# One order for all transfers, an earlier second inverse, and narrowing moved between engines, in a fused RWKV-7 and SoLU kernel

## The chip, the cores and the metric

One core of one Trainium2 chip. The metric is device time in microseconds (us) of one execution; medians are over three or more runs. Each kernel's times are set against runs of the kernel before on the same chip in the same session, as a ratio: the medians of the kernel before are 728.7 to 732.0 us from session to session, so a difference between the medians of two experiments of different sessions is good to some 2 or 3 us.

## The reference, cut to what matters

```python
batch, n_heads, seq, head_dim = (4, 8, 768, 40)
for t in range(S):                                   # attention block
    y[:, :, t] = np.einsum('bhd,bhde->bhe', rt, state)
    Sa = np.einsum('bhde,bhe->bhd', state, at)
    state = state * wt[:, :, None, :] - np.einsum('bhd,bhe->bhde', Sa, bt) + np.einsum('bhd,bhe->bhde', vt, kt)
# then, on the (3072, 320) result x, d_ff = 1024:
h = x @ w_in
solu = h * softmax(h)
out = ((solu - mu) / np.sqrt(var + 1e-06) * g_ln) @ w_out
```

`w_in` and `w_out` arrive as 64-bit floats; the kernel fetches their bits and narrows them to fp32 itself.

## The kernel before

The sequence is cut into 12 chunks of 64 steps, each done in two **rounds** (24 rounds). A chunk needs the inverse of a triangular matrix. Its blocks go to DRAM and come back in another layout (`scatter`, `gather`), VectorE inverts them in 30 steps of two instructions (`invert`), and the inverse goes out and back the same way (`bring_inverse`). The dense block (`hidden`, `output`) runs six rounds behind, once the weights are narrowed. Every engine, and SyncE's queue of transfers, does its instructions in the order that the program was written in; `turns` interleaves generators by a string of letters.

```python
def narrow(dst, land, tmp):                  # 26 pieces of weights
    ...
    yield
    nc.scalar.activation(out=scale, ...); nc.scalar.activation(out=frac, ...)
    nc.scalar.activation(out=rest, in_=low.bitcast(U32), func=AF.Copy, scale=2.0 ** -52)      # L169
    yield
    nc.vector.scalar_tensor_tensor(out=scale, in0=hi, ...)                                    # L171
    yield
    nc.gpsimd.tensor_tensor(out=frac, in0=frac, in1=rest, op=ALU.add)                         # L174
    nc.gpsimd.tensor_tensor(out=dst, in0=frac, in1=scale.bitcast(FP32), op=ALU.mult)          # L175
    yield
...
def front(i):        # ahead of the matmuls of round i
    nc.gpsimd.tensor_copy(out=keyed(a)..., in_=by_heads(given(i, "a")))                       # L361
def attend(i):
    nc.gpsimd.tensor_copy(out=lamv[:, :, :, L:], in_=given(i, "v")...)                        # L446
...
EARLY = ("r r a r W f r W W I r y W r W I a f a W s a f a W I W f s W I f a W L f", ...)      # rounds 0 to 5
STEADY = "r b r a r f b b o r o I o r o y o r I o h a f L a s a h f a I h f s h f h a f h"    # rounds 6 on
...                  # the loop over rounds, cut
if i % 2: gather((i + 3) // 2)
bring_inverse(i + 1)
if i % 2 == 0: load((i + 6) // 2, "w", "a"); parts["L"] = later((i + 6) // 2)   # L loads b, k
turns(...)
```

W is a step of narrowing, I a step of the inverse, f and g the fronts, a `attend`, r the recurrence, L the load of b and k. Small PSUM tiles come from one pool, `bank`, of two buffers that take turns: this matters below.

## Time and profile before

| | before |
|---|---|
| median of three runs | 730.19 us (728.36 to 730.9) |
| first inverse starts, ends (T0) | 24.3, 44.5 us |
| next three inverses end (T1, T2, T3) | 91.1, 151.4, 206.8 us |
| pu of round 0, round 7 starts | 56.6, 264.6 us |
| a pair of rounds in the steady stage | 47.5 us |

These are marks from the timeline: the copy to `ut` that ends each inverse, and the matmuls `pu`, one set a round. I use them throughout, as they cut the 728.0 us of the profiled execution into a start, a stage bound by latency (to about 265 us), a steady stage bound by TensorE, and a tail. Each kernel has one profile, so a mark has a spread too.

### The profile page before, as it was taken

What the parts mean: (1) busy time and instruction counts of PE and PEld (TensorE: products, weight loads), DVE (VectorE), ACT (ScalarE), POOL (GpSimd) and SP (SyncE); (2) the same over time, 40 slices, a digit from 0 to 9 for tenths busy, and PEclk for the clock granted to TensorE, in tenths of its full rate; (3) what the DMA queues carried; (4) which work ended last, traced back from release to release, by engine and by line L of the source; (5) the groups of instructions that cost most, each with busy time, mean ns of one, the idle gap of its engine ahead of it and who ended that gap; (6) DMA issues with size and microseconds to landing.
All of it is one profiled execution on the core that took longest, in us unless ns stands there. A gap on an engine that the chain in (4) does not pass through costs nothing.

```text
span 728.0 us, 25509 instructions
## 1 busy us (share of the span) xinstructions
PE 605.3 (83%) x10873; PEld 431.6 (59%) x10873; DVE 467.5 (64%) x1258; ACT 267.2 (37%) x631; POOL 128.5 (18%) x228
## 2 busy tenths in 40 slices
PE   6436636665766899999999999999999899979997
PEld 4325525554554766677667676767677666645554
DVE  3565945855854678868868688696786763233442
ACT  4114333443441344343524443345334343322322
POOL 4104131332330111220212111220111000000000
PEclk9657576775876799999999999999999999998999
DMA  8946374455444443563555546536315231000001
GB/s 143 160 81 113 72 163 84 83 117 111 92 93 98 67 97 72 103 120 69 100 98 91 101 79 114 102 62 131 71 31 104 53 60 34 21 24 18 19 5 32
DMA packets 269793, 59.84 MB, mean 82 GB/s; under 512 B 255464, under 2 KB 265328, under 8 KB 269680
## 3 DMA queue, kind: packets, MB, share of 16 engines
q1 hardware_dynamic: 265680, 52.73, 39.8%
q10 hardware_dynamic: 4000, 5.48, 2.9%
q8 instruction: 86, 1.41, 0.8%
q14 instruction: 27, 0.22, 0.1%
HBM read 40.08 MB, written 13.37 MB: 73 GB/s over the span
## 4 chain that ended last, share of the span: by engine, by line
PE 58%; DVE 22%; DMA 7%; issue 5%; ACT 4%; SPq 3%; POOL 1%; ACTq 0%; DVEq 0%; POOLq 0%
PE po L662 14%; PE h L617 12%; DVE prod L414 7%; DVE u L416 6%; PE pyo L589 4%; PE plnT L657 3%; PE pcx L341 2%; PE pcum L328 2%; DVE nmax L627 2%; PE plamv L280 2%; PE py L484 2%; DMA raw_b<-in_b_dram 2%; PE pyo L511 2%; PE pvT L261 2%; PE ppsi L280 1%
## 5 line engine op out<-in xcount | busy, mean ns | idle before, releaser
L617 PE MATMUL h<-w_in,xT 128*128 128x512 f32 (+1 forms) x288 | 128.2, 635 | 3.9 <-DVE e L634 3.9
L662 PE MATMUL po<-w,lnT 128*128 128x320 f32 x384 | 114.8, 438 | 0.0
L414 DVE TENSOR_TENSOR prod<-blk,u 128x30 f32<-128x30 f32 (+4 forms) x360 | 107.0, 297 | 11.8 <-DMA blk<-blk_dram 1.0
L416 DVE TENSOR_TENSOR u<-u,prod 128x30 f32<-128x30 f32 (+4 forms) x360 | 101.5, 282 | 12.4
L662 PEld LDWEIGHTS po<-w,lnT 128*128 128x128 f32 x384 | 68.8, 190 | 26.2 <-issue 2.9
L331 POOL TENSOR_TENSOR kx<-raw_b,inv 128x320 f32<-128x320 f32 x24 | 20.7, 866 | 254.8 <-ACT inv L329 210.1
L627 DVE TENSOR_REDUCE nmax<-h 128x1 f32<-128x1024 f32 x24 | 29.3, 1221 | 44.8 <-PE h L617 44.8
L617 PEld LDWEIGHTS h<-w_in,xT 128*128 128x128 f32 (+1 forms) x288 | 38.2, 191 | 31.6 <-issue 29.7
L484 PE MATMUL py<-tinv,nt 32*32 32x32 f32 x768 | 20.6, 202 | 34.2 <-DMA tinv<-ut_dram 34.2
L667 ACT ACTIVATE osb<-po,rs 128x320 f32<-128x320 f32 x24 | 12.7, 527 | 97.2 <-PE po L662 86.4
L596 DVE TENSOR_TENSOR x<-pyo,kx 128x512 f32<-128x512 f32 x24 | 16.6, 690 | 45.2 <-PE pyo L589 44.5
L282 DVE TENSOR_TENSOR lamv<-plamv,cst 128x512 f32<-128x512 f32 x24 | 16.5, 689 | 39.8 <-PE plamv L280 39.8
L649 POOL TENSOR_TENSOR rs<-c,mhalf 128x1 f32<-128x1 f32 x24 | 13.2, 548 | 158.4 <-DVE c L648 158.4
L658 ACT COPY lnT<-plnT 128x512 f32<-128x512 f32 x48 | 27.6, 586 | 33.8 <-PE plnT L657 33.5
L631 ACT ACTIVATE e<-h,nmax 128x1024 f32<-128x1024 f32 x24 | 26.7, 1114 | 36.1 <-DVE nmax L627 36.1
L484 PEld LDWEIGHTS py<-tinv,nt 32*32 32x32 f32 x768 | 17.2, 112 | 36.7 <-issue 29.3
L634 DVE TENSOR_TENSOR e<-h,e 128x1024 f32<-128x1024 f32 x24 | 29.4, 1225 | 14.6 <-ACT e L631 14.2
L499 ACT ACTIVATE tinvT<-pz 32x256 f32<-32x256 f32 x48 | 17.9, 372 | 56.9 <-PE pz L484 56.6
L341 PEld LDWEIGHTS pcx<-cst,lw 128*128 128x128 f32 x192 | 29.1, 209 | 14.9 <-ACT y_mid L496 8.5
L341 PE MATMUL pcx<-cst,lw 128*128 128x132 f32 x192 | 33.6, 307 | 5.3 <-ACT y_mid L496 3.4
L657 PE MATMUL plnT<-cst,e 128*128 128x128 f32 x192 | 29.9, 285 | 5.7 <-DVE e L634 5.4
L575 POOL TENSOR_TENSOR sm<-tot,fac 128x320 f32<-128x320 f32 x20 | 14.8, 742 | 95.2 <-DVE tot L574 79.2
(104 smaller groups left out, 1121.3 us busy)
## 6 DMA issues: line engine op xcount, KB each, us to landing
blk<-blk_dram SPq DMA_DIRECT2D x24, 256.0 KB
raw_w<-in_w_dram SPq DMA_DIRECT2D x24, 160.0 KB
raw_a<-in_a_dram SPq DMA_DIRECT2D x24, 160.0 KB
raw_b<-in_b_dram SPq DMA_DIRECT2D x24, 160.0 KB
raw_k<-in_k_dram SPq DMA_DIRECT2D x24, 160.0 KB
v<-in_v_dram SPq DMA_DIRECT2D x24, 160.0 KB
r<-in_r_dram SPq DMA_DIRECT2D x24, 160.0 KB
out_dram<-osb SPq DMA_DIRECT2D x24, 160.0 KB
```

The costliest lines, as they stand in the source:

```text
L341: nc.tensor.matmul(t[:, g * 132:g * 132 + 132], lhsT=pair(lw, 2 * j + g), rhs=cst[:, lo:lo + 132], start=True, stop=True)
L414: nc.vector.tensor_tensor(out=t, in0=nb[:, j:j + 1, j + 1:Q].to_broadcast([P, rows, m]), in1=u[:, 0:rows, j:j + 1].to_broadcast([P, rows, ...
L416: nc.vector.tensor_tensor(out=u[:, 0:rows, j + 1:Q], in0=u[:, 0:rows, j + 1:Q], in1=t, op=ALU.subtract)
L484: nc.tensor.matmul(t[quarter(out), c:c + Q], lhsT=lhs(p, g), rhs=rhs(p, g), start=True, stop=True)
L589: nc.tensor.matmul(t[half(p), c, g * W:g * W + used], lhsT=kb[half(c), j, 2 * g + p, :], rhs=lam[half(c), h % 2, h // 2, 0:used], start=i ...
L617: nc.tensor.matmul(h[:, j * 512:j * 512 + 512], lhsT=of_round[i // 2]["xT"][rows, kt, i % 2 * P:i % 2 * P + P], rhs=w_in[rows, 4 if kt == ...
L627: nc.vector.tensor_reduce(out=nmax, in_=h, axis=AX.X, op=ALU.max, negate=True)
L631: nc.scalar.activation(out=e, in_=h, func=AF.Exp, bias=nmax, accum_out=esum)
L634: nc.vector.tensor_tensor(out=q, in0=h, in1=e, op=ALU.mult)
L657: nc.tensor.transpose(out=t[:, j * P:(j + 1) * P], in_=q[:, f * P:(f + 1) * P], identity=ident)
L658: nc.scalar.copy(out=lnT[:, fs.start:fs.stop].rearrange("p f t -> p (f t)"), in_=t)
L662: nc.tensor.matmul(o[:, 0:DM], lhsT=lnT[:, f, :], rhs=w2[:, f, :], start=f == 0, stop=f == NF - 1)
```

## The change

The intent: put what the chain waits for ahead of bulk in one queue, use VectorE's idle time while the first inverse travels, and take work off GpSimd, beside whose multiplies a step on VectorE took 0.90 us instead of 0.28. The diff, cut to its core:

```diff
-        nc.scalar.activation(out=rest, in_=low.bitcast(U32), func=AF.Copy, scale=2.0 ** -52)
-        nc.gpsimd.tensor_tensor(out=frac, in0=frac, in1=rest, op=ALU.add)
-        nc.gpsimd.tensor_tensor(out=dst, in0=frac, in1=scale.bitcast(FP32), op=ALU.mult)
+        nc.vector.scalar_tensor_tensor(out=frac, in0=low.bitcast(U32), scalar=2.0 ** -52, in1=frac, op0=ALU.mult, op1=ALU.add)
+        nc.vector.tensor_tensor(out=dst, in0=frac, in1=scale.bitcast(FP32), op=ALU.mult)
 ...
-                nc.scalar.dma_start(out=to[row:row + part.shape[0]], in_=part)      # weights
+                nc.sync.dma_start(out=to[row:row + part.shape[0]], in_=part)        # three pieces ahead, not two
 ...
-        nc.gpsimd.tensor_copy(out=keyed(a)[:, :, :, 0:D], in_=by_heads(given(i, "a")))
+        nc.scalar.copy(out=keyed(a)[:, :, :, 0:D], in_=by_heads(given(i, "a")))
-        nc.gpsimd.tensor_copy(out=lamv[:, :, :, L:], in_=given(i, "v")...)
+        nc.scalar.copy(out=lamv[:, :, :, L:], in_=given(i, "v")...)
 ...
-    EARLY = ("r r a r W f r W W I r y W r W I a f a W s a f a W I W f s W I f a W L f", ...
+    EARLY = ("r r a W I r f W r r I W y r W a f L a I W s a f W a f I W s I f a W f", ...
 ...                       # start: both queues for the first loads; r, a and three pieces of weights ahead of scatter(0)
+        load(0, "w", "b", "a", by=both)
+        turns("f W g", {}, f=f, g=g, W=ws)
+        load(0, "r")
+        load(1, "a")
 ...                       # second inverse right behind the first
+        turns("I W I s s", dict(I=[6, 6]), s=so, I=inv, W=ws)
 ...                       # in the loop: the inverse comes back ahead of the next blocks and of bulk
+            if i == LAG:
+                steps(ws, 99)
+                parts["o"] = centre()          # centring; in the kernel before the last of the W steps, in round 5
+            if more and (i % 2 or i == 0):
+                bring_inverse(i + 1)
             if i % 2 and (i + 3) // 2 < NCH:
                 gather((i + 3) // 2)
+            if i % 2 and i + 2 < N:            # after the round
+                bring_inverse(i + 2)
```

More of the change, by code (lines that the diff above doesn't have):

```diff
@@ L164, in narrow @@
         nc.vector.tensor_scalar(out=man, in0=hi, scalar1=0xFFFFF, scalar2=None, op0=ALU.bitwise_and)
-        frac, rest = man.bitcast(FP32), low.bitcast(FP32)
+        frac = man.bitcast(FP32)
         yield
@@ L172, in narrow @@
                                        op1=ALU.bitwise_or)
-        yield
-        nc.gpsimd.tensor_tensor(out=frac, in0=frac, in1=rest, op=ALU.add)
-        nc.gpsimd.tensor_tensor(out=dst, in0=frac, in1=scale.bitcast(FP32), op=ALU.mult)
+        nc.vector.scalar_tensor_tensor(out=frac, in0=low.bitcast(U32), scalar=2.0 ** -52, in1=frac, op0=ALU.mult,
+                                       op1=ALU.add)
+        nc.vector.tensor_tensor(out=dst, in0=frac, in1=scale.bitcast(FP32), op=ALU.mult)
         yield
     def weights():
-        nc.scalar.dma_start(out=g_rows, in_=moe_g_ln.rearrange("(c p) -> c p", p=P))
+        nc.sync.dma_start(out=g_rows, in_=moe_g_ln.rearrange("(c p) -> c p", p=P))
         pieces, hw, hm = [], DFF // 2, DM // 2
@@ L201, in weights @@
                 land += [x[:, 0:256], x[:, 256:512]]
-            temps = [two.tile([P, 2, 256], I32, tag=tag, name="parts", bufs=1) for tag in ("osb", "parts")]
+            temps = [two.tile([P, 2, 256], I32, tag=tag, name="parts", bufs=n)
+                     for tag, n in (("osb", 1), ("parts", 1), ("xT", 4), ("xT", 4))]
         def fetch(j):
@@ L210, in fetch @@
             for part in parts:
-                nc.scalar.dma_start(out=to[row:row + part.shape[0]], in_=part)
+                nc.sync.dma_start(out=to[row:row + part.shape[0]], in_=part)
                 row += part.shape[0]
-        for j in range(2):
+        for j in range(3):
             fetch(j)
@@ L218, in weights, with centre @@
         for j, (dst, _) in enumerate(pieces):
-            new = None if exact else narrow(dst, land[j % 4], temps[j % 2])
-            for _ in range(2):
-                for part in (open_, new):
-                    if part:
-                        next(part)
-                if _:
-                    fetch(j + 2)
-                yield
-            open_ = new
-        for _ in range(2):
+            new = None if exact else narrow(dst, land[j % 4], temps[j % 4])
+            if new:
+                next(new)
+            yield
+            if new:
+                next(new)
             if open_:
                 next(open_)
+            fetch(j + 3)
+            yield
+            open_ = new
+        if open_:
+            next(open_)
+        yield
+    def centre():
         pg = bank("pg")
@@ L233, in weights @@
         nc.scalar.copy(out=g_col, in_=pg[:, 0:NF])
-        yield
         gb = two.tile([P, NF, P], FP32, tag="e", name="gb", bufs=1)
@@ L237, in weights @@
         yield
-        mean = bank("mean")
+        t = bank("mean")
         for c in range(NF):
-            nc.tensor.matmul(mean[:, 0:DM], lhsT=gb[:, c, :], rhs=w2[:, c, :], start=c == 0, stop=c == NF - 1)
+            nc.tensor.matmul(t[:, 0:DM], lhsT=gb[:, c, :], rhs=w2[:, c, :], start=c == 0, stop=c == NF - 1)
+        mean = two.tile([P, DM], FP32, tag="osb", name="mean", bufs=1)
+        nc.scalar.copy(out=mean, in_=t[:, 0:DM])
         yield
@@ L243, in weights @@
             nc.vector.scalar_tensor_tensor(out=w2[:, c, :], in0=w2[:, c, :], scalar=g_col[:, c:c + 1],
-                                           in1=mean[:, 0:DM], op0=ALU.mult, op1=ALU.subtract)
+                                           in1=mean, op0=ALU.mult, op1=ALU.subtract)
             if c % 2:
@@ L290, with load @@
     of_round = [dict() for _ in range(NCH)]
-    def load(n, *names):
+    def load(n, *names, by=(nc.sync, nc.sync)):
         if n >= NCH:
@@ L305, in load @@
             for c in range(2):
-                nc.sync.dma_start(out=to[half(c)], in_=ap[2 * c:2 * c + 2, :, n * L:(n + 1) * L, :]
+                by[c].dma_start(out=to[half(c)], in_=ap[2 * c:2 * c + 2, :, n * L:(n + 1) * L, :]
                                   .rearrange("b h t d -> t (b h) d"))
@@ L445, in attend @@
         lamv = d["lamv"] = wide("lamv", L + D, 2)
-        nc.gpsimd.tensor_copy(out=lamv[:, :, :, L:], in_=given(i, "v").rearrange("q (m z) d -> q z m d", z=2)[:, :, :, 0:D])
+        nc.scalar.copy(out=lamv[:, :, :, L:], in_=given(i, "v").rearrange("q (m z) d -> q z m d", z=2)[:, :, :, 0:D])
         kT = transposed("kT", d["kb"][:, 0])
@@ L690, in fronts @@
         return [j for j in ((4, 5) if i == 0 else (i + AHEAD,)) if j < N]
-    EARLY = ("r r a r W f r W W I r y W r W I a f a W s a f a W I W f s W I f a W L f",
-             "r r a r W f g r W W I r y W r W I a f g a W s a f g a W I W f g s W I f g a W L f g")
+    EARLY = ("r r a W I r f W r r I W y r W a f L a I W s a f W a f I W s I f a W f",
+             "r r a W I r f W r r I g W y r I W a f g L W a I a f g W I s a f g a W I f g s W I f g W I")
     STEADY = "r b r a r f b b o r o I o r o y o r I o h a f L a s a h f a I h f s h f h a f h"
-    front_of = {}
-    front_of = {}
-    front_of = {}
-    front_of = {}
     front_of = {}
@@ L714, in inverse_steps @@
     def inverse_steps(i):
-        if i < 3:
-            return [[8, 8, 8, 8], [0, 3, 4, 3], [6, 6, 5, 5]][i]
+        if i == 0:
+            return [3, 2, 2, 3, 3, 3, 3, 1]
         if i < LAG:
-            return [0, 5, 5, 4] if i % 2 else [5, 5, 4, 4]
+            return [0, 0, 6, 6, 5 if i < LAG - 1 else 2] if i % 2 else [4, 4, 4, 3, 0]
         return [0, 7, 7] if i % 2 else [6, 7, 5]
@@ L726 @@
     with tc.manual_schedule():
-        load(0, "w", "a", "b", "k")
-        f, g = front(0), front(1)
+        both = (nc.sync, nc.scalar)
+        load(0, "w", "b", "a", by=both)
+        load(0, "k", "v")
+        f, g, at, inv, so, ws = front(0), front(1), attend(0), invert(0), solve(0), weights()
         turns("f g", {}, f=f, g=g)
-        load(1, "w", "a")
+        load(1, "w")
+        turns("f W g", {}, f=f, g=g, W=ws)
+        load(0, "r")
+        load(1, "a")
+        turns("f f f f g g g g f g", {}, f=f, g=g)
+        f, g = front(2), front(3)
         turns("f g", {}, f=f, g=g)
+        scatter(0)
         load(1, "b")
-        turns("f f f f g g g g f g", {}, f=f, g=g)
-        scatter(0)
         gather(0)
-        load(0, "v", "r")
         load(1, "k")
-        f, g, at, inv, so, ws = front(2), front(3), attend(0), invert(0), solve(0), weights()
-        turns("f g f g f f g g", {}, f=f, g=g)
-        load(2, "w", "a", "b", "k")
-        turns("a a I a a W", dict(I=99), a=at, I=inv, W=ws)
+        turns("a f g W a a W f f a g g W a", {}, f=f, g=g, a=at, W=ws)
+        load(2, "w", "a")
+        turns("I f g f g I f g", dict(I=[8, 8]), f=f, g=g, I=inv)
+        load(1, "v", "r")
+        scatter(1)
+        load(2, "b", "k")
+        gather(1)
+        turns("I a", dict(I=99), a=at, I=inv)
         bring_inverse(0)
-        turns("a f g a f g f g", {}, f=f, g=g, a=at)
-        scatter(1)
-        gather(1)
-        load(1, "v", "r")
         begin(0)
-        turns("s s", {}, s=so)
         inv = inverses()
+        turns("I W I s s", dict(I=[6, 6]), s=so, I=inv, W=ws)
         after, before = None, None
@@ L752 @@
             m, more, js = i - LAG, i + 1 < N, fronts(i)
+            now = hidden(m) if m >= 0 else None
+            parts = dict(r=recurrence(i), y=readout(i), I=inv, W=ws, h=now, b=after, o=before)
+            if i == LAG:
+                steps(ws, 99)
+                parts["o"] = centre()
+            parts.update(zip("fg", (front_of[j] for j in js)))
+            if more:
+                parts.update(a=attend(i + 1), s=solve(i + 1))
+            if more and (i % 2 or i == 0):
+                bring_inverse(i + 1)
             if i % 2 and (i + 3) // 2 < NCH:
                 gather((i + 3) // 2)
-            now = hidden(m) if m >= 0 else None
-            parts = dict(r=recurrence(i), y=readout(i), I=inv, W=ws, h=now, b=after, o=before)
-            if i >= LAG:
-                steps(ws, 99)
-            parts.update(zip("fg", (front_of[j] for j in js)))
-            if more:
-                bring_inverse(i + 1)
-                parts.update(a=attend(i + 1), s=solve(i + 1))
             if i % 2 == 0:
@@ L767 @@
             if i % 2:
+                if i + 2 < N:
+                    bring_inverse(i + 2)
                 load((i + 3) // 2, "v", "r")
```

## The prediction

> **What bounds the kernel now.** I read the page first, then busy time by windows, then the chain of waits, then the timelines of the transfer queue and of VectorE. The page's slices cut the 728.0 us into stages (one digit is 18.2 us):
>
> ```profile
> PE   6436636665766899999999999999999899979997
> DVE  3565945855854678868868688696786763233442
> DMA  8946374455444443563555546536315231000001
> ```
>
> TensorE is at 9 from slice 15 on, and at 3 to 7 before it. The windows put numbers to that:
>
> ```profile
> core 0: us, PE busy (x) PEld busy (x) DVE busy (x) ACT busy (x) POOL busy (x), PEclk, DMA share, GB/s
> 45.00:57.00 12.00, 8.37 (x184) 7.10 (x188) 4.24 (x9) 3.99 (x10) 0.00 (x0) 0.64 0.47 84
> 57.00:93.00 36.00, 22.33 (x436) 18.16 (x428) 29.58 (x87) 14.44 (x37) 11.07 (x15) 0.71 0.51 98
> 93.00:127.00 34.00, 17.13 (x399) 14.26 (x392) 17.25 (x48) 12.68 (x33) 10.66 (x15) 0.70 0.61 122
> 127.00:153.00 26.00, 18.51 (x404) 15.11 (x396) 22.07 (x65) 11.70 (x33) 9.30 (x16) 0.67 0.37 74
> 318.00:365.00 47.00, 46.09 (x916) 32.85 (x915) 36.33 (x97) 19.39 (x45) 7.96 (x14) 1.00 0.50 91
> ```
>
> From about 270 us two rounds take 47.5 us and TensorE is busy 46.1 of 47: that stage is bound by matmuls which the change leaves alone. Before it no engine is full; the chain there is latency. So **the change can win only ahead of about 265 us**. My milestones, from the timeline, are the ends of the inverses (the copy to ut, L420) at 44.5, 91.1, 151.4, 206.8 and 261.2 us, and the starts of the matmuls pu (L550), one set a round, at 56.6, 92.4, 126.5, 153.1, 184.8, 208.5, 244.7 and 264.6. Inverse ends are 60.3 and 55.4 us apart here, against 47.5 later. The queue of SyncE shows why:
>
> ```profile
> 91.13 0.54 SPq L423 DMA_DIRECT2D u_dram<-u  x1
> 91.79 0.59 SPq L425 DMA_DIRECT2D ut_dram<-ut  x1
> 92.43 0.55 SPq L423 DMA_DIRECT2D u_dram<-u  x1
> 93.07 2.38 SPq L306 DMA_DIRECT2D raw_b<-in_b_dram  x2
> 95.55 3.62 SPq L306 DMA_DIRECT2D raw_k<-in_k_dram  x2
> 99.26 2.74 SPq L389 DMA_DIRECT2D blk_dram<-nt  x4
> 103.49 1.12 SPq L396 DMA_DIRECT2D blk<-blk_dram  x2
> 109.32 1.79 SPq L436 DMA_DIRECT2D tinv<-ut_dram  x4
> 111.16 1.93 SPq L439 DMA_DIRECT2D tinvT<-u_dram  x4
> ```
>
> The inverse goes out at 91.1 to 93.0 and comes back only from 109.3, with raw_b, raw_k and the next blocks between. The next inverse waits for blk and starts at 107.1, 16 us after the last ended; pu of round 2, which needs tinvT, starts at 126.5, 35.4 us after. A second loss is on VectorE:
>
> ```profile
> 31.33 0.28 DVE L416 TENSOR_TENSOR u<-u,prod 128x120 f32<-128x120 f32 x1
> 31.65 0.90 DVE L414 TENSOR_TENSOR prod<-blk,u 128x114 f32<-128x114 f32 x1
> L174 POOL TENSOR_TENSOR parts<-parts,bits 128x160 f32<-128x160 f32 (+1 forms) x26 | 16.5, 636 | 3.4 <-ACT bits L169 3.4
> L175 POOL TENSOR_TENSOR w_in<-parts 128x256 f32<-128x256 f32 x10 | 8.3, 829 | 28.9 <-DVE parts L171 28.5
> ```
>
> A step of the inverse takes 0.28 us alone and 0.90 where a GpSimd multiply (from 31.56) runs beside it.
>
> **What the Trainium skill says.** "SBUF — State Buffer", section "SBUF: two separate sides": VectorE, when it has two SBUF inputs, and GpSimd lock one port pair for a whole instruction, and the loser blocks. The trace agrees: 0.28 to 0.90. Summing, over VectorE's instructions ahead of 245 us, duration less the shortest of the same shape, 13.3 us fall on those beside the narrowing's L174 and L175, and about 3.4 on those beside L331. "DMA: Bandwidth & Descriptors", section "Issuing engines are not separate DMA queues": transfers of all issuing engines interleave on the same 16 DMA engines, and several issuers save issue time alone. So one queue loses no bandwidth as such; what the change decides is who stands ahead of whom. Same page, "Queues, rings and completion order": descriptors are consumed in ring order. The trace agrees: in the first 17 us the 160-byte packets of seven loads run back to back at about 1,030 a us (1 us for each half of a load), and the first blocks' 128-byte packets start only behind them.
>
> **Part by part.**
> (1) Start. In the order of instructions, the changed kernel sends k, v, the second w, three pieces of weights (128 packets of 2 KB each, about 1 us a piece in the packet rates), r and the second a ahead of the first blocks: 16 halves and three pieces, about 19 us, against 14 halves now. Further, ScalarE, now the copier of a, stands in order ahead of lw of the second front, of kT, vT and rT, so it waits there for the second a. Working: loads from 2.4 us; a, spread over two queues, lands at about 9.5; the second w waits for lw (10.5); the second a lands at about 22; then ScalarE has some fourteen pieces of 0.4 to 0.6 us up to rT, 28.5; lamv on VectorE, which the order puts ahead of the first inverse, 30.5 to 31. So the first inverse starts at about 31, not 24.3: +6.7 us. In it now stand two kx and two nt (4 x 0.68 = 2.7), which before lay in the shadow of the return trip: it ends at 54.4, not 44.5. Return and solve as before, 12.1 us: first pu at 66.5, +10 us.
> (2) Second inverse. In those 12 us VectorE was busy 4.24; now it does the set-up (1.2), 14 of the 30 steps (about 8) and parts of narrowing. From lamu (70.5) to the end of the inverse remain sixteen steps (9), x, sm, psi, lamv, two kx, two nt (5.3) and some four pieces of narrowing (7): 22, with stalls 25. So T1 is about 96 against 91.1: **what is won here does not quite pay for the start**.
> (3) Inverse ahead of bulk. After T1: u and ut out (2), four scatters (2), eight returns at 0.48 (4), blk (1.1 and about 3 to land): the third inverse starts at T1 + 12 instead of + 16. VectorE from T1 to T2, by its order: a bare inverse 18.7, two rounds' own products 9.0, narrowing 11.6 (seven pieces of 0.47 to 0.57 and 0.93 to 1.22): 39.3. Of these 6.7 fit ahead of T1 + 12; 32.6 follow, at 87% busy (now 85% in 127 to 153): 37. T2 - T1 = 49 against 60.3. The same for T3 - T2: 13.5 to the start, 30 of work after it, 48 against 55.4. T3 is 96 + 97 = 193 against 206.8.
> (4) Narrowing. 26 pieces lose 33 us of GpSimd, 9.6 of ScalarE (L169) and 13.3 of contention. VectorE gains a multiply-add (0.41 or 0.31, as L171) and a multiply (about 0.4 or 0.31, by the slope of L414): 10 x 0.81 + 16 x 0.62 = 18. For VectorE that is a net cost of 5, so no gain in itself. It is spread thinner, about 3.5 pieces a round against 5.5 to 6, and three pieces are left for the start of round 6.
> (5) Centring. The mean (L240, 6.1 us of TensorE at 217.8, all on the chain) leaves round 5 and goes into round 6, behind its pu, with 8 x 0.54 of VectorE. From T3 to pu of round 7 I get 33 (three late pieces included) and 25 (19.9 now, plus some 5): 58, as now (57.8).
> Sum: pu of round 7 at 193 + 58 = 251 against 264.6, a gain of 13.6, and the rest is the steady stage and the tail, unchanged: 716.6. I take 2.5 off, as the stalls that I left at today's share also fall when fewer weight transfers are issued by ScalarE (about 40 of 0.38 us): **714 us**.
>
> **The rivals.**
> (a) The slow start eats everything: if a lands later still or gather waits behind the weights, the first pu comes at 75 and the kernel at 725 to 732. For it speaks the DMA share of 0.79 and 0.90 in the first 45 us; against it, that the steps' hand-set counts look tuned to fit.
> (b) The start is no slower, because two queues carry the first loads faster (up to 1,300 packets a us elsewhere in the trace), and the filled return trip counts fully: T1 near 85, 703 to 706. For it: VectorE idle in that trip. Against: the a copy on ScalarE.
> (c) VectorE becomes the bound ahead of 250 us by its 5 us net and three late pieces; then pairs take 52 to 54 and the time is about 724.
> (d) ScalarE, with two more copies of 0.45 a round, delays TensorE in the steady stage. TensorE idles only 0.9 of 47 us there, so 0.2 us a round would cost 4: 718. Against: ScalarE is busy 19.4 of 47.
>
> **Range and chances.** The sum's weak terms are the start (+10, give or take 5) and each pair's 49 and 48 (give or take 4 each, correlated); together about 10 us. Low 700 is rival (b) with quicker pairs, high 728 is (a). The border for faster by over 2% is 715.6, close to the centre: 0.54 faster, 0.42 same, 0.04 slower.
>
> **What would show it.** Right: inverse ends near 54, 96, 145 and 193; returns of the inverse issued within 5 us after it goes out; VectorE's steps at 0.28 but beside L337 (kx); 47.5 us a pair after 270. Wrong: step 1, if the first inverse starts before 27; step 2, if T1 is below 90; step 3, if the return still waits behind loads or T2 - T1 is over 54; step 5, if round 6 takes over 32; the frame itself, if a pair in the steady stage leaves 47 to 48.

## The result, and the profile after

Median 721.54 us (718.5 to 724.68, 4 runs) against 729.3 in the same rounds; the ratio is 0.9892, 95% interval 0.9844 to 0.9940: 1.1% faster, clear of noise, but under 2% and so called the same. A ratio here and below is the mean time of one kernel's runs over that of the other's of the same rounds, so not quite the ratio of the medians.

| mark | before | predicted | after |
|---|---|---|---|
| first inverse starts | 24.3 | 31 | 31.8 |
| T0 | 44.5 | 54.4 | 52.7 |
| pu of round 0 | 56.6 | 66.5 | 64.0 |
| T1 | 91.1 | 96 | 90.1 |
| T2 | 151.4 | 145 | 140.5 |
| T3 | 206.8 | 193 | 193.3 |
| pu of round 7 | 264.6 | 251 | 248.1 |
| a pair in the steady stage | 47.5 | 47.5 | 48.7 |
| end of the profiled span | 728.0 | | 719.9 |

At pu of round 7 the changed kernel leads by 16.5 us, at the end by 8.1: **half of the gain is given back, most of it in the steady stage**, where nothing was meant to change. Rounds 7 to 19 took 285.8 us before (264.6 to 550.4) and take 292.6 now (248.1 to 540.7), 6.8 more; the other 1.6 go in the tail.

The page's busy times and slices after:

```profile
PE 606.7 (84%) x10873; PEld 428.9 (60%) x10873; DVE 468.7 (65%) x1310; ACT 275.1 (38%) x654; POOL 77.7 (11%) x128
PE   4524866767658899999999999999999899979997
DVE  2387969658656959687687596786876754232442
DMA  9964553743765353545554626545325131000001
```

GpSimd fell from 128.5 to 77.7 us, and TensorE's 13th slice rises from 6 to 8. Busy time by windows, for three of the stretches shown before (columns: window, its length, then busy time of PE, PEld, DVE, ACT, POOL, then clock, DMA share, GB/s):

```profile
45.00:57.00 12.00, 0.00 (x0) 0.00 (x0) 7.34 (x29) 2.53 (x7) 0.00 (x0) 0.50 0.84 164
93.00:127.00 34.00, 22.52 (x481) 18.46 (x484) 25.75 (x84) 11.82 (x31) 2.03 (x3) 0.70 0.43 84
318.00:365.00 47.00, 45.45 (x910) 32.36 (x910) 34.36 (x93) 20.24 (x49) 6.47 (x10) 1.00 0.52 95
```

In 45 to 57, the return trip of the first inverse before, TensorE now does nothing at all: the first inverse ends only at 52.7. In 93 to 127 VectorE is busy 25.75 us instead of 17.25, and TensorE 22.52 instead of 17.13: here the change wins. In 318 to 365 TensorE is busy 45.45 instead of 46.09. SyncE's queue around T1:

```profile
88.66 0.55 SPq L429 DMA_DIRECT2D u_dram<-u  x1
90.77 0.33 SPq L431 DMA_DIRECT2D ut_dram<-ut  x1
91.14 0.55 SPq L429 DMA_DIRECT2D u_dram<-u  x1
91.74 2.35 SPq L395 DMA_DIRECT2D blk_dram<-nt  x4
94.20 3.22 SPq L442 DMA_DIRECT2D tinv<-ut_dram  x4
97.52 1.88 SPq L445 DMA_DIRECT2D tinvT<-u_dram  x4
99.44 1.13 SPq L402 DMA_DIRECT2D blk<-blk_dram  x2
```

The inverse comes back from 94.2, 3.4 us after ut went out, where it was 17.5 before (91.8 to 109.3); the next inverse starts at 102.9, T1 + 12.8, where the prediction worked out T1 + 12.

**Where the steady stage loses.** I cut TensorE's work of ten rounds into blocks, start to next start. Every block is the same to 0.03 us a pair but three: pu (+0.65), pcum (+0.41) and plnT (+0.11), together +1.17, against +1.12 for the pair. The timelines at that point of a round, ScalarE and then TensorE, before:

```profile
383.96 0.46 ACT L324 ACTIVATE lw<-raw_w 128x320 f32<-128x320 f32 x1
384.32 0.57 ACT L542 COPY sT<-psT 128x512 f32<-128x512 f32 x1
384.79 0.60 ACT L263 COPY kT<-pkT 128x512 f32<-128x512 f32 x1
383.94 0.75 PE L550 MATMUL pu<-tinvT,x 64*64 64x64 f32 x32
384.95 0.81 PE L328 MATMUL pcum<-lw,cst 128*128 128x320 f32 x2 [0.27 <-ACT sT L542]
```

and after:

```profile
370.35 0.46 ACT L330 ACTIVATE lw<-raw_w 128x320 f32<-128x320 f32 x1
370.71 0.45 ACT L367 COPY a<-raw_a 128x320 f32<-128x320 f32 x1
371.06 0.58 ACT L548 COPY sT<-psT 128x512 f32<-128x512 f32 x1
371.54 0.47 ACT L452 COPY lamv<-v 128x320 f32<-128x320 f32 x1
371.89 0.59 ACT L269 COPY kT<-pkT 128x512 f32<-128x512 f32 x1
370.32 0.75 PE L556 MATMUL pu<-tinvT,x 64*64 64x64 f32 x32
371.69 0.81 PE L334 MATMUL pcum<-lw,cst 128*128 128x320 f32 x2 [0.62 <-ACT sT L548]
```

The two copies stand among sT and kT: sT starts 0.71 us after lw instead of 0.36, kT 1.54 instead of 0.83. pcum takes over the bank that sT empties, and waits 0.62 us instead of 0.27; plnT takes over the one that kT empties. So pcum starts 1.37 us after pu instead of 1.01. That is an argument from waits. The first two experiments test whether the copies make the loss; no run tests the step through the buffers alone (a third buffer in `bank`, say).

### The profile page after: what moved, and what is told of

It is laid out like the page before. It is cut to its first block, busy times and chain, and to the rows that moved or that the text cites. A ratio compares the mean times of both kernels' runs of the same rounds, so it can differ in the third digit from the quotient of the medians. Undisturbed runs are those within 1.5% of the kernel's fastest.

```text
span 719.9 us, 25430 instructions
## 1 busy us (share of the span) xinstructions
PE 606.7 (84%) x10873; PEld 428.9 (60%) x10873; DVE 468.7 (65%) x1310; ACT 275.1 (38%) x654; POOL 77.7 (11%) x128
## 4 chain that ended last, share of the span: by engine, by line
PE 54%; DVE 21%; DMA 8%; ACT 7%; issue 5%; SPq 5%; ACTq 0%; DVEq 0%
PE po L668 15%; PE h L623 10%; DVE u L422 6%; DVE prod L420 5%; PE pyo L595 4%; PE plnT L663 4%; PE pcx L347 3%; PE pcum L334 2%; DVE nmax L633 2%; DMA ut_dram<-ut 2%; PE ppsi L286 2%; DMA blk<-blk_dram 2%; PE plamu L286 2%; PE pyo L517 2%; PE plamv L286 2%
## 5 line engine op out<-in xcount | busy, mean ns | idle before, releaser
L422 DVE TENSOR_TENSOR u<-u,prod 128x30 f32<-128x30 f32 (+4 forms) x360 | 96.5, 268 | 12.3
L420 DVE TENSOR_TENSOR prod<-blk,u 128x30 f32<-128x30 f32 (+4 forms) x360 | 93.5, 260 | 11.5 <-DMA blk<-blk_dram 1.0
L668 PEld LDWEIGHTS po<-w,lnT 128*128 128x128 f32 x384 | 69.0, 190 | 26.2 <-issue 2.9
L347 PEld LDWEIGHTS pcx<-cst,lw 128*128 128x128 f32 x192 | 29.8, 214 | 19.4 <-ACT y_mid L502 15.2
L267 PE MATMUL pbT<-cst,kx 128*128 128x128 f32 x96 | 17.9, 321 | 25.8 <-ACT tinvT L505 18.7
L640 DVE TENSOR_TENSOR e<-h,e 128x1024 f32<-128x1024 f32 x24 | 29.4, 1225 | 14.8 <-ACT e L637 14.3
L334 PE MATMUL pcum<-lw,cst 128*128 128x320 f32 x48 | 23.2, 572 | 18.4 <-ACT lw L330 9.0
L663 PE MATMUL plnT<-cst,e 128*128 128x128 f32 x192 | 31.4, 294 | 6.2 <-DVE e L640 5.4
L288 DVE TENSOR_TENSOR lamv<-plamv,cst 128x512 f32<-128x512 f32 x24 | 16.5, 689 | 27.3 <-PE plamv L286 27.2
L267 PEld LDWEIGHTS pbT<-cst,kx 128*128 128x128 f32 x96 | 12.3, 163 | 35.4 <-issue 35.4
L663 PEld LDWEIGHTS plnT<-cst,e 128*128 128x128 f32 x192 | 22.1, 147 | 18.3 <-ACT kT L269 6.6
```

The source lines that it names most:

```text
L267: nc.tensor.transpose(out=t[:, g * P:(g + 1) * P], in_=pair(src, g), identity=ident)
L334: nc.tensor.matmul(t[:, 0:DM], lhsT=c_("cum_in"), rhs=lw[:, :, 0:D], start=True, stop=True)
L347: nc.tensor.matmul(t[:, g * 132:g * 132 + 132], lhsT=pair(lw, 2 * j + g), rhs=cst[:, lo:lo + 132], start=True, stop=True)
L420: nc.vector.tensor_tensor(out=t, in0=nb[:, j:j + 1, j + 1:Q].to_broadcast([P, rows, m]), in1=u[:, 0:rows, j:j + 1].to_broadcast([P, rows, ...
L422: nc.vector.tensor_tensor(out=u[:, 0:rows, j + 1:Q], in0=u[:, 0:rows, j + 1:Q], in1=t, op=ALU.subtract)
L640: nc.vector.tensor_tensor(out=q, in0=h, in1=e, op=ALU.mult)
```

## The experiments

Twelve kernels, all correct. The edits are against the changed kernel unless told otherwise.

| run | edit | median us | ratio to before | 95% |
|---|---|---|---|---|
| the change | | 721.5 | 0.9892 | 0.9844 to 0.9940 |
| e1 | copies back on GpSimd | 711.3 | 0.9750 | 0.9725 to 0.9775 |
| e2 | *before*, copies on ScalarE | 732.1 | 1.0030 | 1.0001 to 1.0060 |
| e3 | narrowing as before | 715.9 | 0.9792 | 0.9757 to 0.9826 |
| e4 | e1, weights later at the start | 719.6 | 0.9840 | 0.9789 to 0.9891 |
| e5 | bulk ahead of the inverse | 726.0 | 0.9939 | 0.9917 to 0.9962 |
| e6 | second inverse not ahead of round 0 | 725.7 | 0.9940 | 0.9916 to 0.9964 |
| e7 | weights' transfers on ScalarE | 728.0 | 0.9959 | 0.9923 to 0.9995 |
| e8 | e1, another start | 719.3 | 0.9826 | 0.9768 to 0.9884 |
| e9 | centring at once | 726.7 | 0.9972 | 0.9932 to 1.0013 |
| e10 | e1 and e3 | 709.2 | 0.9718 | 0.9689 to 0.9747 |
| e11 | e10, the other start again | 714.1 | 0.9789 | 0.9753 to 0.9826 |
| e12 | narrowing twice as dense | 735.2 | 1.0075 | 1.0046 to 1.0104 |

### The copies: e1 and e2

```diff
-        nc.scalar.copy(out=keyed(a)..., ...);  nc.scalar.copy(out=lamv[..., L:], ...)
+        nc.gpsimd.tensor_copy(out=keyed(a)..., ...);  nc.gpsimd.tensor_copy(out=lamv[..., L:], ...)
```

> The changed kernel with the two copies (a, and v into lamv) back on GpSimd. Theory A (ScalarE's two added copies stand in front of sT and kT at each round's start and hold TensorE at pu and pcum): the steady pair goes from 48.7 back to 47.5 us, and the start is 1 to 3 us earlier since ScalarE no longer waits there for the second a; the whole near 709 to 712. Rival B (the steady loss comes from the new order of the transfers, or from the placing of the returns of the inverse): the pair stays at 48.7 and the whole at 719 to 721.

Measured: 711.26 us, ratio 0.9750. The steady pair is 47.5 us again, and the wait of pcum is what it was:

```profile
367.71 0.75 PE L556 MATMUL pu<-tinvT,x 64*64 64x64 f32 x32
368.73 0.81 PE L334 MATMUL pcum<-lw,cst 128*128 128x320 f32 x2 [0.27 <-ACT sT L548]
```

pu of round 7 is at 247.9, the changed kernel's 248.1: of the 9.6 us between the two profiles, 6.4 come from rounds 7 to 19 and 2.9 from the tail. The tail is not shown to be the copies' doing. From pu of round 19 to the end it takes 179.2 us in the changed kernel and 176.3 in e1, but 176.3 also in e3, where the copies stay on ScalarE, and moving the copies in the kernel before leaves it at 177.4 (177.6 without them). The first inverse started at 29.4 instead of 31.8, which lies within the spread of that mark, and pu of round 0 came only 0.6 us earlier.

e2 makes the opposite edit on the kernel before.

> The kernel before with only the two copies moved to ScalarE. Theory A: the steady pair goes from 47.5 to 48.7 us, the whole from 729 to 737 or later. Rival B: pair 47.5, whole within 2 us of 729.

Measured: the pair went from 47.5 to 48.7 us, the very number, and rounds 7 to 19 from 285.8 to 292.6. So **the two copies alone make the loss of the steady stage**, whatever the order of transfers. The whole moved less than theory A said, and hardly more than rival B, to 732.07 (ratio 1.003; the profiled span 732.4 against 728.0): the stage ahead of round 7 became 2.2 us shorter in the profile. Why was not followed up.

### The order of returns: e5

```diff
-    EARLY = (... "r y W a f L a I W s ..." ...)      # L ahead of the inverse's end
+    EARLY = (... "r y W a f a I W s ... W L f" ...)  # L behind it
+            if more: bring_inverse(i + 1)            # at each round's start, behind gather
-                    bring_inverse(i + 2)             # not after odd rounds
```

> The changed kernel with the loads of b and k (and the next blocks) back ahead of the returns of the inverse, as in the kernel before. If the step is worth what the prediction said (11 us for the first pair of inverses, 7 for the next), inverse ends lie 58 to 61 and 54 to 56 us apart instead of 50.4 and 52.8, and the whole goes to 727 to 737. Rival: VectorE's own work sets the distance, then under 3 us are lost.

Measured: 725.97 us, 4.4 more (0.0047 in the ratios, and the two intervals together leave some 0.005 either way, so the time alone is at the edge of noise). Inverse ends lie 52.8 and 55.5 us apart instead of 50.4 and 52.8. The second distance is that of the kernel before (55.4), the first is far from its 60.3: the order of returns is worth about 5 us, and most of what T2 - T1 gained has another source. This fell between the two theories. (The profiled execution was the slowest of its four, 729.49, so the distances are the better measure.)

### The second inverse: e6

```diff
-        turns("I W I s s", dict(I=[6, 6]), s=so, I=inv, W=ws)
+        turns("W s s", {}, s=so, W=ws)
-            return [3, 2, 2, 3, 3, 3, 3, 1]
+            return [6, 5, 4, 4, 4, 4, 4, 1]
```

> The changed kernel without the twelve steps of the second inverse ahead of round 0 (they are spread over round 0 instead). If filling the return trip of the first inverse is what paid, the second inverse ends 5 to 8 us later than 90.1 and the whole is 4 to 8 us longer. Rival: VectorE has room in round 0 anyway, then under 2 us.

Measured: T1 94.2 instead of 90.1, of which 1.5 us were there at T0, ahead of the edit; from T0 to T1 it took 40.1 us instead of 37.4 (36.4 to 37.1 in e1, e4, e5 and e9). The whole is 725.72, 4.2 more, again at the edge of noise (0.0048 in the ratios). So filling the return trip pays, some 3 to 4 us: the first theory's direction, at or under the lower edge of its range.

### Narrowing: e3 and e12

```diff
-        nc.vector.scalar_tensor_tensor(out=frac, in0=low..., scalar=2.0 ** -52, in1=frac, ...)
-        nc.vector.tensor_tensor(out=dst, in0=frac, ...)
+        # low word on ScalarE as before, then
+        nc.gpsimd.tensor_tensor(out=frac, in0=frac, in1=rest, op=ALU.add)
+        nc.gpsimd.tensor_tensor(out=dst, in0=frac, in1=scale..., op=ALU.mult)
```

> The changed kernel with the narrowing's last two steps back on GpSimd and the low word back on ScalarE. The prediction's step 4: VectorE loses 18 us of work and takes on some 13 of contention, so the whole stays within 3 us of 721.5 and T2 - T1 within 2 of 50.4. Rival: freeing VectorE of GpSimd's lock is what shortened the inverses (with the bulk ahead T2 - T1 was still 52.8 against 60.3 in the kernel before, so 7.5 us have another source); then T2 - T1 goes to 55 or more and the whole to 727 to 731.

Measured: 715.87, 5.7 less, which neither theory had. From T1 to pu of round 7 it took 153.8 us instead of 158.0, although T1 fell 1.4 us later. VectorE's two added steps cost 20.0 us in the changed kernel (L172 10.0, L174 5.2 and 4.8), while in e3 VectorE's instructions beside GpSimd's narrowing were 8.3 us longer in sum than the shortest of their shape, not 13.3. In the changed order, then, the two steps cost VectorE 11.7 us net. Of the 5.8 us between the two profiles, though, 2.8 were won by pu of round 7 and 2.9 are the shorter tail that e1 showed too.

```diff
-            turns(..., dict(I=inverse_steps(i)), **parts)
+            turns(..., dict(I=inverse_steps(i), W=2), **parts)
```

> The changed kernel with two steps of narrowing at each place of the early rounds instead of one (14 to 16 a round; the kernel before had 11 to 13, the changed one has 7 to 8). If the thinner spread is part of the gain, T1 and T2 - T1 grow by 2 to 4 us each and the whole by 3 to 8. Rival: VectorE's total is the same, only earlier, and the late pieces before round 6 go away: within 2 us, or faster.

Measured: 735.21, 13.7 more, beyond both. T1 is 97.9 and T2 - T1 69.3 instead of 50.4 (T3 - T2 then 44.4). The queue of SyncE behind T1 shows one thing that happened:

```profile
107.42 1.13 SPq L402 DMA_DIRECT2D blk<-blk_dram  x2
108.64 24.01 SPq L211 DMA_DIRECT2D bits<-in_moe_w_out_dram  x8
132.71 2.23 SPq L442 DMA_DIRECT2D tinv<-ut_dram  x4
```

Eight pieces of weights stood in SyncE's order ahead of the second return of the inverse, and the last five had to wait, by the program for their landing buffers: 24 us. (In the changed kernel three pieces stand there for 11.24 us.) So the thin spread matters: **in a hand-made order a transfer that waits holds all behind it**. How much of the 13.7 is this and how much VectorE's load was not separated.

### Weights' transfers: e7

```diff
-                nc.sync.dma_start(out=to[...], in_=part)      # weights and g_rows
+                nc.scalar.dma_start(out=to[...], in_=part)
```

> The changed kernel with only the weights' transfers issued by ScalarE again, in the same places of the program. If issuing from SyncE is what pays (some 40 issues of 0.38 us off ScalarE), the whole grows by 3 to 6 us, with T2 - T1 longer by 2 or more. Rival: ScalarE has room, and the weights no longer stand between SyncE's own transfers, then within 2 us of 721.5, or faster.

Measured: 727.95, 6.4 more in the medians, 0.7% in the ratios; T1 is 94.2, T2 - T1 52.2, T3 - T2 54.5. Keeping them off ScalarE pays, as the first theory said, but its reason, the issue time, is the smaller part. There are 32 such issues of some 0.38 us, 12 us in all, while ScalarE stood 62 us in sum right in front of them, 14.7 us at the longest (some of it may have cost nothing):

```profile
48.39 0.40 ACT L168 ACTIVATE parts<-parts 128x256 f32<-128x256 int32 x1
63.46 2.00 ACTq L211 DMA_DIRECT2D bits<-in_moe_w_in_dram  x4
65.51 0.75 ACT L502 COPY y_mid<-py 32x256 f32<-32x256 f32 x2 [16.71 <-DMA bits<-in_moe_w_in_dram]
```

In the kernel before, where ScalarE issued the same transfers two pieces ahead instead of three, this standing is 0.3 us in all. Whether the longer look-ahead alone makes it is not shown. But an engine that issues a transfer that waits stands with it; in the changed kernel that is SyncE, for 33 us in sum.

### Centring: e9

```diff
-                parts["o"] = centre()
+                steps(centre(), 99)
```

> The changed kernel with the centring done at once ahead of round 6 instead of in its gaps. If the move of the centring pays, the whole grows by 4 to 8 us (its matmuls were 6.1 us on the chain before); rival: round 6 is full anyway and nothing is lost, within 2 us of 721.5.

Measured: 726.66, 5.1 more. From pu of round 5 to that of round 6 it took 34.7 us instead of 25.1, from there to round 7 22.6 instead of 25.8: the two rounds together took 6.4 us more, so about that much is hidden by the move.

### Another start: e4, e8 and e11

Three tries to win back the 7 us of the start, on top of e1 (e4, e8) or e10 (e11).

```diff
 # e4: the first fetch of weights goes behind gather(0) and k
-        turns("f W g", {}, f=f, g=g, W=ws)
+        turns("f g", {}, f=f, g=g)
         load(1, "k")
+        turns("W", {}, W=ws)
```

> The changed kernel with both copies back on GpSimd (711.3 measured so) and the first three pieces of weights fetched behind the first blocks and k instead of ahead of r and the second a. They hold the transfer queue for about 3 us (1 us each), so the first inverse starts at 26 to 27 instead of 29.4, the first pu at 60 to 61 instead of 63.4, and the whole falls to 708 to 709. Rival: narrowing, later by as much, gives it back: 711.

Measured: 719.6, 8 us worse than e1 (0.9% in the ratios). The first inverse started at 36.3, not 26 to 27: the first two pieces are narrowed ahead of it in VectorE's order, and VectorE stood 13 us for them:

```profile
29.63 0.75 DVE L162 TENSOR_SCALAR parts<-bits 128x256 int32<-128x256 int32 x1 [12.98 <-DMA bits<-in_moe_w_in_dram]
```

I had moved the fetch and not its user.

```diff
 # e8: blocks first, then the rest; the inverse ahead of psi and lamv
+        scatter(0); gather(0); load(1, "a"); load(0, "r"); ...; load(1, "b"); load(1, "k"); turns("W", {}, W=ws)
+        turns("a f g a I W a W f f a g g I W a", dict(I=[8, 5]), ...)
```

> The changed kernel with both copies back on GpSimd and another start: first blocks out and back ahead of the second a, r, b, k and the weights, and the first inverse on VectorE ahead of psi and lamv. The first inverse should start at 23.5 to 25 instead of 29.4 and end at 46.5 to 48.5 instead of 52.2, the first pu at 58 to 60, the whole at 706 to 708. Rival: the second blocks or r arrive too late and hold the first inverse or round 0, then 710 to 713.

Measured: 719.3. The inverse started at 26.2 but ended at 56.4: after eight steps VectorE stood 4.5 us for a piece of weights (36.03), with ScalarE's rT behind the same piece. The same mistake. e11 leaves the narrowing out there, on top of e10:

```diff
+        turns("a f g a I a f f a g g I a", dict(I=[8, 5]), ...)
```

> The same with the start tried before (first blocks ahead of bulk, first inverse ahead of psi and lamv), but with no narrowing in VectorE's and ScalarE's order until the first inverse is out; in that trial the inverse started at 26.2 and stood 4.5 us at a piece of weights that had not landed, and ScalarE's rT behind it. Expected: first inverse from 26 to 47-49, first pu at 58 to 60, the whole 701 to 704. Rival: rT and lamv still come late and hold it, then 706 to 709.

Measured: 714.1. The start is as hoped, first inverse 24.3 to 48.9, and T1 85.5 instead of e10's 89.4. But T2 - T1 is 54.0 (e10: 50.0) and T3 - T2 55.4 (52.2), and pu of round 7 comes at 252.1 against 244.6: all is given back, and more. The narrowing now runs three steps behind in every round; that this shifts some wait into the chain is my guess, and it stays open.

### The best version: e10

> The changed kernel with both copies and the last two steps of the narrowing back on GpSimd, all transfers as changed. If the two parts are independent (copies -10.3 us, narrowing -5.7 against 721.5), 705 to 707 us; rival: they meet on GpSimd and lock VectorE, then 709 or more.

Measured: 709.19 us, ratio 0.9718 (0.9689 to 0.9747), steady pair 47.5: faster than both kernels by more than their intervals. Against e1 the narrowing on GpSimd adds little here (711.3 to 709.2; the intervals overlap), less than e3's 5.7: the number is the rival's, 709 or more. The profiles give another reason than the rival's lock. Ahead of round 7 the narrowing on GpSimd wins 3.3 us here against e1 (244.6 against 247.9) and 2.8 in e3; the other 2.9 of e3 are the shorter tail, which e1 has already. So ahead of round 7 and in the steady stage the two parts do add up.

## Why the prediction was right or wrong, point by point

The time, 721.54 us, lies in the range of 700 to 728, 7.5 above the centre; the likeliest class (faster, 0.54) did not come, the second (same, 0.42) did. Ahead of round 7 the sum was right and its terms were not: 16.5 us were won where 16.1 were forecast (730.2 less 714), but T1 came 5.9 us earlier than worked out, T2 - T1 was 1.4 longer, T3 - T2 4.8 longer, and T3 to pu of round 7 3.2 shorter. That T3 came out at 193.3 for 193 is luck. The miss of 7.5 is then, in the main, the 6.8 us of the steady stage.

- **The frame, that only the stretch ahead of 265 us can change: wrong, and by the prediction's own sign (a pair outside 47 to 48).** The steady pair went from 47.5 to 48.7. It was named as rival (d), with 0.2 us a round and 4 in all; it is 0.56 a round and 6.8 up to round 19. The reason given against it, that ScalarE is busy only 19.4 of 47 us, is the step that failed: what counted was where the copies stand in ScalarE's order, among two results that free banks for TensorE. Less these 6.8 us the kernel would have come to about 714.7 (an estimate by subtraction); e1 measured 711.3, with the shorter tail.
- **Step 1, the start: right in its parts.** The second a landed as worked out, and ScalarE's copy of it began at 22.11; the first inverse started at 31.8 (31), ended at 52.7 (54.4). ScalarE's wait is not the only cause: with the copies off ScalarE lamv was done at 24.2, but then the first inverse waited 5.14 us for the blocks and started at 29.4. The trace given for ring order tests nothing: in the kernel before, the blocks were issued from 16.30, their first packet moved at 17.17, and the last packet of the loads had ended at 16.61.
- **Step 2, the second inverse: T1 mis-sized by 6 us** (96 against 90.1). The second inverse did pay for the slow start; e6 gives the filled return trip 3 to 4.
- **Step 3, inverse ahead of bulk: the first distance was right (50.4 for 49), the second mis-sized (52.8 for 48), the attribution wrong.** T3 - T2 fell by 2.6 us, not 7.4. The inverse that ends at T3 started 14.5 us after T2 (13.5) and took 38.3 from there (34.5). e5 gives the order of returns 2.4 us of the first distance's gain of 9.9, and all of the second's. Weights on SyncE give 1.8 and 1.7 (e7); where the rest of the 9.9 comes from is not shown, as e12 changes the spread of the narrowing and the queue at once. The prediction summed VectorE's work and so had a distance without knowing whose it was.
- **Step 4, narrowing: mis-sized.** The two steps cost VectorE 20.0 us, not 18, and the contention that their move removes in the changed order was 8.3 (e3), not the 13.3 of the order before: net 11.7, not 5. It shows in the time, about 3 us ahead of round 7 (e3, e10). Also, the pair of lines shown for the contention, 0.28 and 0.90, stands beside kx (L331, 31.56), which both kernels leave on GpSimd, and not beside the narrowing.
- **Step 5, centring: its stretch mis-sized.** T3 to pu of round 7 is 54.8, not 58 as before; e9 gives the move 5 us.
- Rivals: (a) and (b) each had a piece (slow start; quick T1). (c) came in part: pairs of inverses are 50.4 and 52.8 us apart, the second in its range of 52 to 54, and by e3 VectorE's net load costs time.

So gains were met by two losses. Of the gains, each shown by undoing one part, those of e7 and e9 (5 to 6 us; 0.0067 and 0.0080 in the ratios, give or take 0.006) are just clear of noise in the times; those of e5 and e6 (about 4) are clear in the distances alone. The losses are the copies, 6.4 to 6.8 us in the steady stage, and the narrowing on VectorE, about 3 ahead of round 7. Undoing parts one at a time does not give numbers that sum to the 8 us between the kernels.

## What to carry to other kernels

Before work moves to an engine with room, look at what stands behind it there in program order: two copies of 0.45 and 0.47 us a round, on an engine busy 43% of the time, cost the busiest one 0.56 us a round, and the waits say that PSUM buffers came free later. When a transfer moves in a queue, move its user too, and ask what waits behind it if its buffer is not free. Keep a check on stages that "cannot change": 6.8 us of a gain of 16.5 were lost in one. And before two profiles' marks are compared, find out how far a mark moves where the program is the same.

## What the Trainium skill lacked or had wrong

- "DMA: Bandwidth & Descriptors", section "Issuing engines are not separate DMA queues", says that several issuing engines only save the sequencer's issue time, "which is usually small relative to the DMA itself". Here it mattered which sequencer stands still: weights on one engine or the other made 6.4 us in the medians, 0.7% in the ratios (e7), with ScalarE standing 62 us in front of them where their issues take 12; and pieces that waited held SyncE's queue for 11.24 us in the changed kernel and 24.01 in e12. The section does not draw that consequence.
- "Perfetto Trace Analysis", section "Optimizing Scalar/DVE Operations", suggests moving work to Scalar or even GPSIMD when DVE is saturated, and warns of DVE and GPSIMD alone that it might not help. Here a move from GpSimd to ScalarE, far from full (20.2 of 47 us), lengthened a pair of rounds by 1.12 us. The section does say that engines which aren't saturated can cause bubbles on others, but not that an offload to one can make them. Between VectorE and GpSimd, where it doubts the use, a move did pay: two steps put on GpSimd brought 8.3 us of contention and took 20.0 of work off VectorE (e3).
- "SBUF — State Buffer" agrees with the trace where it was used (0.28 against 0.90 us); no run here was found to be against it.
